# Attention and channel mix on one core: q, k and p laid out channels first, v as its tiles lie, and four output blocks stored channels first

## The chip, the core and the metric

The kernel runs on one core of a Trainium2 chip. The metric is the device time of one execution in microseconds. TensorE (PE) multiplies, VectorE (DVE) and ScalarE (ACT) do the elementwise work, GpSimd (POOL) sets constants, and SyncE (SP) issues nearly all transfers. Each engine works through its own queue in order; an instruction waits until the ones of other engines that it names are done.

## The reference

Eight batches of eight heads with 576 positions of 64 channels. Per head, 32 packed rows p attend to k and v; then q attends to what came out. The heads side by side (512 channels) go through a channel mix: two mixtures with the position before, one matrix with a squared ReLU and a second matrix behind it, and a sigmoid gate.

```python
def sm_attn(qq, kk, vv):
    s = scale * np.matmul(qq, kk.transpose(0, 1, 3, 2))
    a = np.exp(s - np.max(s, axis=-1, keepdims=True))
    a = a / (np.sum(a, axis=-1, keepdims=True) + 1e-09)
    return np.matmul(a, vv)
p_packed = sm_attn(p, k, v)
out = sm_attn(q, p_packed, p_packed)     # (8, 8, 576, 64) -> x (8, 576, 512)
xk = mu_k * x + (1.0 - mu_k) * x_prev    # x_prev: one position earlier
xr = mu_r * x + (1.0 - mu_r) * x_prev
k = np.maximum(xk @ w_k, 0.0)            # 512 -> 1024
v = k * k @ w_v                          # 1024 -> 512
r = 1.0 / (1.0 + np.exp(-(xr @ w_r)))
return (r * v).astype(np.float32)
```

## The kernel before

The 4608 positions are nine blocks of 512. A float32 product is made of three matmuls of a high and a low half: operand and weight are each split into two tiles (names ending in `h` and `l`). The first five blocks are done one by one (`gates`, `keys`, `values`: lines 1158 to 1160, 1091 to 1093, 1187 to 1189); the last four are two pairs, whose products come from sums and differences of quarters (`products_of`, line 1491), stored channels first on the chip and turned back before they are stored.

The attention of a batch runs in between. `front`: first scores of p and k (line 728; kT and qT hold two heads, channels on the partitions), maximum (801), exp (808), a turn of the weights by blocks of 32 with a way through memory (`weights_moved`, 851: `away`, then `aT`), weighted sum of v (750), pm (774) and its transpose (780). `scores` and `back`: second scores (884), softmax on DVE and ACT (900 to 923), product with pm (931), a copy into xt (954). Batch 0 has versions of its own (`first_side` and others, lines 568 to 663 and 977).

Loads before: q and k come in natural order. Batch 0's pairs of heads are transposed on PE (475, 506) and copied out by DVE and ACT (480, 483, 511, 514). For the other batches, four loads of 32 partitions with 32 channels each fill a `raw` tile (three of them), and DVE transposes it by 32 x 32 blocks into a `kq` tile (four of them, line 460). Positions are then in another order, which exp of batch 1 and the copy into xt undo. p goes the same way (533, 554). v comes in one or two, from batch 2 on in four loads for half a batch.

The weights are unpacked on the chip from 8-byte numbers (`convert`: ACT lines 342, 344, 356, DVE lines 347 and 358), 20 pieces.

What sets the order: the class `Flow` plays the program through while it is built, with estimated durations, and writes each engine's queue in the order in which steps become due; rank numbers decide between steps that are due (the table of numbers below). Tiles come from pools of slots (`take`, `give`): a step that takes a slot waits for the last user of it. Until the first gates are under way, `fill` puts matmuls of 128 columns on a constant into PE's queue wherever the play shows PE free (line 1859, tile `spare`).

The end: for a pair's output, DVE multiplies by the gate (1722, 1725), transposes by blocks (1732), and four stores per output tile of 128 channels write 32 x 16 x 32 pieces (`load`, line 245, is used for all transfers). The last tile of all is multiplied in two parts (1749), turned by PE (1756), copied by ACT and DVE (1760, 1763) and stored.

Of the kernel before, what the change touches and what calls it, by code (L numbers as in the profile page):

```python
# [8 lines left out]
F32 = mybir.dt.float32  # L9
# [4 lines left out]
AX = mybir.AxisListType  # L14

# [165 lines left out]

@with_exitstack
def attn_pack_channel_mix(ctx: ExitStack, tc: tile.TileContext, q, k, v, p, mu_k, mu_r, w_k, w_v, w_r, out):
    nc = tc.nc
    B, H, S, D = q.shape
    NP = p.shape[2]
    DM, DF = w_k.shape
    P = 128
    NG = H // 4
    NPR = H // 2  # L190
# [15 lines left out]
    FIRST = 12.453, 12.081, 16.585, 10.332  # L206
    RANK_1, RANK_MIX, RANK_KEYS, RANK_R, RANK_W, RANK_W2, RANK_V, LOADS_1, RANK_SQ, RANK_REST, HOLD_V, HOLD_S = 14.383, 2.279, 9.364, 21.382, 11.434, 11.544, 16.223, 19.391, 0.152, -6.533, 0.05, 0.25
    RANK_LATE1 = -1.021
    RANK_LATE2 = 7.09
    RANK_LATE3 = 9.434  # L210
    RANK_LATE4 = 10.248
    RANK_LATE5 = 2.56
    RANK_LATE6 = 9.599
    RANK_LATE7 = 3.494
    RANK_LATE8 = 20.327
    RANK_LATE9 = 10.578
    RANK_LATE10 = 7.095
    RANK_LATE11 = 3.446
    RANK_LATE13 = 29.829
    RANK_LATE14 = 4.595  # L220
    RANK_LATE12 = 8.964
# [30 lines left out]
    LATER, MARGIN = 1.2, 0.8  # L252
# [3 lines left out]
    def reached():  # L256
# [3 lines left out]
    RUNS = ((0, 5), (5, 5), (10, 4), (14, 4)), ((0, 4), (4, 4), (8, 5), (13, 5))  # L260
    MOVED = 2
    EARLY = 1
# [7 lines left out]
    BUFS = dict(raw=3, kq=4, vt=2, pt=1, a0=1, a1=1, aT=1, pm=2, e=3, a2=1, xt=6, tmp=4, xk=NC, sq=NF, sig=4,  # L270
                pa=2, both=1, m=4, n=4, staged=4, ex=3, pair=0, ring=0, store=4, twin=0)
# [7 lines left out]
    PAIRS = NB - 4, NB - 2  # L279
    MORE = {("sig", 4 + j): f"raw{j}" for j in range(3)}  # L280
    MORE.update({("sig", 7): "a20", ("tmp", 4): "ex2"})
    RANK_B, RANK_TURN, RANK_BACK, RANK_OUT, RANK_L = 0.2, 1.444, 1.061, 2.193, 44.75
    RANK_SUMS = dict(k=32.198, v=22.02, r=12.77)
    CHAINS = dict(A=(10.632, 0.893), B=(37.5, 6.511), R=(38.068, 6.0))
# [9 lines left out]
    for tag, n, size in (  # L294
        ("xk", NC, 2 * TB), ("sq", NF, 2 * TB), ("tmp", 4, WP), ("sig", 4, DM), ("kq", 4, S), 
        ("raw", 3, S), ("a2", 1, S), ("ex", 3, TB), ("e", 3, S), ("aT", 1, 5 * P), ("vt", 2, NPR * 5 * D),
    ):
        for j in range(n):
            sb.tile([P, size], F32, name=tag, tag=f"{tag}{j}")
# [71 lines left out]
    def first_pair(src, tag, j, space):  # L371

        slot = yield from flow.take(space)
        raw = tile_([P, 6, 2 * D], F32, space, slot, "raw")
        for hh in range(2):
            yield from load(
                raw[:T6, :, hh * D:(hh + 1) * D], src[0, 2 * j + hh].rearrange("(c p) d -> p c d", p=T6), 0.51, 0.6,
            )
            back_to_issue()
        if tag == "kT":  # L380
            flow.spawn(transposed_on_pe(tag, 0, j, space, slot, raw), RANK_LATE7 if j < 2 else RANK_LATE8, flow.free["dma"] + LANDS)
            return
        for hf in range(2):
            flow.spawn(
                first_transposed(j, hf, space, slot, raw), RANK_LATE9 if j < 2 else RANK_LATE10, flow.free["dma"] + LANDS
            )

    def first_loads():
        flow.spawn(first_packed(), 5)
        for h in range(2):  # L390
            for j in (2 * h, 2 * h + 1):
                flow.spawn(first_pair(k, "kT", j, "xk"), FIRST_K[h])
                flow.spawn(first_pair(q, "qT", j, "xk" if j == NPR - 1 else "sq"), FIRST_Q[h])
            flow.spawn(values_of(0, h), FIRST_V[h])

    def loads(b):
        flow.spawn(packed(b), lrank(b) - 0.03)
        for src, tag in ((k, "kT"), (v, "vt"), (q, "qT")):
            if tag == "vt":
                for h in range(2):  # L400
                    flow.spawn(values_of(b, h), lrank(b) - 0.01)
                continue
            flow.now.rank = lrank(b) - (0.02 if tag == "kT" else 0.0)
            for pr in range(NPR):

                space = "raw"
                slot = yield from flow.take(space)
                if b < EARLY:

                    raw = tile_([P, 6, 2 * D], F32, space, slot, "raw")  # L410
                    for hh in range(2):
                        yield from load(
                            raw[:T6, :, hh * D:(hh + 1) * D], src[b, 2 * pr + hh].rearrange("(c p) d -> p c d", p=T6),
                            0.51, 0.6,
                        )
                        back_to_issue()
                    flow.spawn(transposed_on_pe(tag, b, pr, space, slot, raw), rank(b), flow.free["dma"] + LANDS)
                    continue

                raw = tile_([P, NTB, 32], F32, "raw", slot)  # L420
                for o in range(0, P, 32):
                    hh, dh = divmod(o // 32, 2)
                    yield from load(
                        raw[o:o + 32],
                        src[b, 2 * pr + hh, :, 32 * dh:32 * dh + 32].rearrange("(t tb) d -> t tb d", tb=NTB),
                        0.63, 0.41,
                    )
                    back_to_issue()
                flow.spawn(transposed(tag, b, pr, slot, raw), rank(b) if b < 3 else RANK_TURN, flow.free["dma"] + LANDS + (LATER if b > 2 else 0.0))
# [4 lines left out]
    def values_of(b, h):  # L434

        slot = yield from flow.take("vt")
        vt = tile_([P, NPR, 5 * D], F32, "vt", slot)
        own = slice(h, H, 2) if b else slice(h * NPR, (h + 1) * NPR)
        if b < MOVED:
            yield from load(  # L440
                vt[:, :, :4 * D], v[b, own, :NQ, :].rearrange("h (p c) d -> p h (c d)", c=4), 0.46, 1.8
            )
            back_to_issue()
            yield from load(vt[:S - NQ, :, 4 * D:], v[b, own, NQ:, :].rearrange("h p d -> p h d"), 0.63, 0.45)
        else:

            own = v[b, h::2].rearrange("h (t tb) d -> t h (tb d)", tb=NTB)
            for j, (first, n) in enumerate(RUNS[h]):
                yield from load(vt[32 * j:32 * j + 32, :, :n * D], own[:, :, first * D:(first + n) * D], 0.46, 0.5)
                if j < 3:  # L450
                    back_to_issue()
        vts[b, h] = slot, vt
        flow.set(("vt", b, h))

    def transposed(tag, b, pr, raw_slot, raw):
        yield from reached()
# [35 lines left out]
    def first_transposed(pr, hf, raw_space, raw_slot, raw):  # L492
# [14 lines left out]
        if hf:  # L507
            flow.give(raw_space, raw_slot)
# [1379 lines left out]
```

## Time and profile before

| | |
|---|---|
| median of 3 runs | 570.71 us (570.67 to 571.06) |
| the profiled run's own time | 569.96 us |
| its span, first to last instruction | 567.8 us |
| PE, DVE, ACT busy | 98%, 83%, 67% of the span |
| first mixing matmul (line 1136) | 32.18 us |
| last matmul of the channel mix (line 1491) | starts at 560.96 us |
| DMA traffic | 86.16 MB, 229091 packets, 183848 of them under 512 B |

How to read it: the span runs from the first to the last instruction of the profiled execution, and all places below are microseconds from its start. In the profile an fp32 matmul of batch 0 or a filler appears as two records. The end of a matmul is modelled, so two that follow each other overlap in the rows; the distance between their starts is what one takes.

### The profile page before, as it was taken

What the parts mean: (1) busy time and instruction counts of PE and PEld (TensorE: products, weight loads), DVE (VectorE), ACT (ScalarE), POOL (GpSimd) and SP (SyncE); (2) the same over time, 40 slices, a digit from 0 to 9 for tenths busy, and PEclk for the clock granted to TensorE, in tenths of its full rate; (3) what the DMA queues carried; (4) which work ended last, traced back from release to release, by engine and by line L of the source; (5) the groups of instructions that cost most, each with busy time, mean ns of one, the idle gap of its engine ahead of it and who ended that gap; (6) DMA issues with size and microseconds to landing.
All of it is one profiled execution on the core that took longest, in us unless ns stands there. A gap on an engine that the chain in (4) does not pass through costs nothing.

```text
span 567.8 us, 10356 instructions
## 1 busy us (share of the span) xinstructions
PE 555.0 (98%) x3642; PEld 431.8 (76%) x3642; DVE 471.8 (83%) x926; ACT 378.8 (67%) x693; POOL 7.2 (1%) x36
## 2 busy tenths in 40 slices
PE   8999999999999999999999999999999999999995
PEld 7867767787787777677777777678888888888884
DVE  3797699937889988977998799994599997879874
ACT  2689979443585776365745668688996738787630
POOL 4000000000000000000000000000000000000000
PEclk9999999999999999999999999999999999999999
DMA  9989765666674865876747773242352483624255
GB/s 214 292 243 283 168 140 122 151 137 127 112 179 127 184 160 126 192 178 186 152 100 235 195 141 115 100 147 75 102 194 63 120 208 77 202 75 148 80 124 94
DMA packets 229091, 86.16 MB, mean 152 GB/s; under 512 B 183848, under 2 KB 217136, under 8 KB 229040
## 3 DMA queue, kind: packets, MB, share of 16 engines
q1 hardware_dynamic: 224624, 84.58, 59.3%
q10 hardware_dynamic: 4160, 0.66, 0.6%
q8 instruction: 29, 0.48, 0.4%
q0 software_dynamic: 256, 0.26, 0.2%
q14 instruction: 22, 0.18, 0.1%
HBM read 62.00 MB, written 23.46 MB: 151 GB/s over the span
## 4 chain that ended last, share of the span: by engine, by line
PE 61%; DVE 19%; ACT 7%; DMA 6%; SPq 4%; issue 3%; DVEq 0%; ACTq 0%
PE ph L1491 31%; SPq L245 4%; PE ph L1091 3%; PE ph L1092 3%; PE ph L1093 3%; PE pvo L1187 3%; PE pvo L1189 3%; PE pvo L1188 3%; DVE x L1058 3%; DMA raw<-in_k 2%; PE pr L1158 1%; PE pr L1159 1%; PE pr L1160 1%; DVE sw L1326 1%; DVE sig L1198 1%
## 5 line engine op out<-in xcount | busy, mean ns | idle before, releaser
L1187 PE MATMUL pvo<-wv_h,sq 128*128 128x512 f32 x160 | 64.4, 403 | 0.2 <-ACT r L1103 0.2
L1091 PE MATMUL ph<-xk,wk_h 128*128 128x512 f32 x160 | 64.4, 402 | 0.0
L1188 PE MATMUL pvo<-wv_l,sq 128*128 128x512 f32 x160 | 62.4, 390 | 0.0
L1092 PE MATMUL ph<-xk,wk_h 128*128 128x512 f32 x160 | 62.4, 390 | 0.0
L1093 PE MATMUL ph<-xk,wk_l 128*128 128x512 f32 x160 | 62.4, 390 | 0.0
L1189 PE MATMUL pvo<-wv_h,sq 128*128 128x512 f32 x160 | 62.4, 390 | 0.0
L954 ACT COPY xt<-pa 128x576 f32<-128x576 f32 x28 | 33.0, 1258 | 15.7 <-PE pa L931 15.7
L1491 PE MATMUL ph<-vT,ring 128*128 128x512 f32 x174 | 43.0, 393 | 0.0
L1058 DVE SCALAR_TENSOR_TENSOR x<-xt,mus,x 128x64 f32<-128x64 f32 (+5 forms) x80 | 34.9, 475 | 6.5 <-ACT x L1054 6.5
L1187 PEld LDWEIGHTS pvo<-wv_h,sq 128*128 128x128 f32 x160 | 30.0, 188 | 12.6 <-issue 5.0
L1054 ACT ACTIVATE x<-xt,mus 128x64 f32<-128x64 f32 (+5 forms) x80 | 35.6, 500 | 5.5 <-DVE sq L1112 2.6
L1103 ACT ACTIVATE r<-ph 128x512 f32<-128x512 f32 x40 | 23.8, 596 | 22.4 <-PE ph L1093 15.8
L1491 PEld LDWEIGHTS ph<-vT,ring 128*128 128x128 f32 x174 | 32.7, 188 | 7.4
L1091 PEld LDWEIGHTS ph<-xk,wk_h 128*128 128x128 f32 x160 | 30.1, 188 | 10.8 <-issue 4.1
L1189 PEld LDWEIGHTS pvo<-wv_h,sq 128*128 128x128 f32 x160 | 30.0, 188 | 6.5
L1093 PEld LDWEIGHTS ph<-xk,wk_l 128*128 128x128 f32 x160 | 30.0, 188 | 6.5
L1188 PEld LDWEIGHTS pvo<-wv_l,sq 128*128 128x128 f32 x160 | 30.1, 188 | 5.6
L1092 PEld LDWEIGHTS ph<-xk,wk_h 128*128 128x128 f32 x160 | 30.1, 188 | 5.6
L1491 PE MATMUL ph<-vB,wv_h 128*128 128x512 f32 x104 | 32.4, 393 | 0.0
L1342 ACT CAST sw<-sw 128x256 fp32r<-128x256 f32 x40 | 15.5, 403 | 20.1 <-DVE sw L1326 8.9
L1344 DVE TENSOR_TENSOR sw<-sw 128x256 fp32r<-128x256 f32 x40 | 16.3, 416 | 15.1 <-ACT sw L1342 15.1
L1110 DVE CAST sq<-r 128x512 fp32r<-128x512 f32 x40 | 16.5, 413 | 13.6 <-ACT r L1106 13.1
(224 smaller groups left out, 1383.0 us busy)
## 6 DMA issues: line engine op xcount, KB each, us to landing
sum<-sw SPq DMA_DIRECT2D x40, 256.0 KB, 2.5
ring<-sum SPq DMA_DIRECT2D x36, 256.0 KB, 3.2
raw<-in_k SPq DMA_DIRECT2D x112, 72.0 KB, 2.8
raw<-in_q SPq DMA_DIRECT2D x112, 72.0 KB, 2.9
out<-sig SPq DMA_DIRECT2D x20, 256.0 KB, 2.7
wv_h<-sum SPq DMA_DIRECT2D x18, 256.0 KB, 3.5
wv_l<-sum SPq DMA_DIRECT2D x18, 256.0 KB, 4.0
st<-in_moe_w_k SPq DMA_DIRECT2D x8, 512.0 KB, 5.6
```

Source lines behind the costliest of these rows:

```text
L245: dict(queue=nc.sync, scalar=nc.scalar, gpsimd=nc.gpsimd)[queue].dma_start(dst, src)
L954: nc.scalar.copy(*in_order(b, xt[:, :, 1 + hf * HS:1 + (hf + 1) * HS], xt[:, :, 1:].rearrange("p c (t a b) -> p c a b t", a=2, t=32)[:, :, ...
L1054: nc.scalar.mul(x32[:, o:o + n], xts[b, c][:, 1 + s:1 + s + n], mus[:, j, c:c + 1])
L1058: nc.vector.scalar_tensor_tensor(x32[:, o:o + n], xts[b, c][:, s:s + n], mus[:, j + 1, c:c + 1], x32[:, o:o + n], op0=ALU.mult, op1=ALU.add,)
L1091: nc.tensor.matmul(ph, wk_h[:, c, fs], xh, start=(c == 0), stop=False)
L1092: nc.tensor.matmul(ph, wk_h[:, c, fs], xl, start=False, stop=False)
L1093: nc.tensor.matmul(ph, wk_l[:, c, fs], xh, start=False, stop=(c == NC - 1))
L1103: nc.scalar.activation(r, ph, AF.Relu)
L1187: nc.tensor.matmul(pv[t], sh, wv_h[:, f, :], start=(n == 0), stop=False)
L1188: nc.tensor.matmul(pv[t], sh, wv_l[:, f, :], start=False, stop=False)
L1189: nc.tensor.matmul(pv[t], sl, wv_h[:, f, :], start=False, stop=(n == NF - 1))
L1491: nc.tensor.matmul(bank[2], w, x, start=(not more and step == k == 0), stop=(step == 2 and k == count - 1), skip_group_check=True,)
```

## The change

The arrays are laid out before the launch, and put together after it. q and k are passed as (8, 4, 128, 576): two heads' channels on the partitions; p as (8, 128, 128); v by half of the heads in the order of the tiles; the shares of mu_k and mu_r by channel. On the chip, kT and qT are loaded as they are used, one load each, into `kq` (seven tiles; `raw` is gone). The transposes of q, k and p on PE and DVE, and the copies behind them, are taken out. pt is loaded for batch 0 in two loads into a zeroed tile. Positions stay in natural order, so exp and the copy into xt write plain rows. v's half batch is one load of 128 rows and one of 64. The last four blocks are stored channels first, one store per tile of 128 channels; the transposes at the end are taken out. The table of ranks has other numbers, and with the count RANK_LATE13 all 20 weight pieces take the other branch of `convert`: ACT's first step goes, and DVE's one step becomes two.

```diff
-    FIRST = 12.453, 12.081, 16.585, 10.332
-    RANK_1, RANK_MIX, ... = 14.383, 2.279, 9.364, 21.382, 11.434, 11.544, 16.223, 19.391, 0.152, -6.533, 0.05, 0.25
-    RANK_LATE13 = 29.829
+    FIRST = 19.125, 23.858, 15.496, 14.378
+    RANK_1, RANK_MIX, ... = 14.138, 6.204, 10.067, 22.577, 16.168, 18.235, 23.505, 24.159, 0.05, -0.644, 0.056, 0.212
+    RANK_LATE13 = 0.991
...
-    BUFS = dict(raw=3, kq=4, vt=2, ...
+    BUFS = dict(kq=7, vt=2, ...
...
+    def turned(src, tag, b, pr):
+        slot = yield from flow.take("kq")
+        t = tile_([P, S], F32, "kq", slot, tag)
+        yield from load(t, src[b, pr], 0.46, 1.0)
...
-                raw = tile_([P, NTB, 32], F32, "raw", slot)
-                for o in range(0, P, 32):
-                    hh, dh = divmod(o // 32, 2)
-                    yield from load(raw[o:o + 32],
-                        src[b, 2 * pr + hh, :, 32 * dh:32 * dh + 32].rearrange("(t tb) d -> t tb d", tb=NTB), ...
+        for pr in range(NPR):
+            flow.spawn(turned(k, "kT", b, pr), lrank(b) - 0.02)
...
-        yield vec(S)
-        nc.vector.transpose(t.rearrange("p (a b) -> p a b", b=32), raw)
...
+        main = v[b, h, :4 * P * NPR * D].rearrange("(p c r d) -> p c r d", p=P, c=4, r=NPR)
+        yield from load(vt[:, :4], main, 0.46, 1.8)
...
-        nc.scalar.copy(*in_order(b, xt[...], xt[...].rearrange("p c (t a b) -> p c a b t", a=2, t=32)[:, :, hf], px))
+        nc.scalar.copy(xt[:, :, 1 + hf * HS:1 + (hf + 1) * HS], px[:, :, :HS])
...
-        nc.vector.transpose(x.rearrange("p (b i) -> p b i", i=32), sig)
-        for a in range(4):
-            yield from load(out[t0:t0 + TB, d * P + 32 * a:d * P + 32 * a + 32]..., x[32 * a:32 * a + 32]..., 0.63, 0.4, queue)
+        yield from load(out[b * TB + d * P:b * TB + (d + 1) * P, :], sig, 0.46, 0.9, queue)
...
-            nc.tensor.transpose(turned[:, at:at + P], sig[:, part.start + at:part.start + at + P], ident)
-            nc.scalar.copy(x, turned)
+        yield from load(out[t0:t0 + P, part], sig[:, part], 0.4, 0.3, "queue" if part.start else "scalar")
```

PE's queue at the start of the program, before the change (`spare` is a filler, `pa<-ident,raw` and `pq<-ident,raw` are transposes of k and q, `pa<-kT,pt` the first scores, `pa<-ident,a` the turn of the weights, `pv` the weighted sum):

```order
L1859 MATMUL spare<-ident 128x128 x10
L475 MATMUL pa<-ident,raw 128x96 x6
L1859 MATMUL spare<-ident 128x128 x3
L475 MATMUL pa<-ident,raw 128x96 x6
L1823 MATMUL pu<-ident,rows 128x8
L1859 MATMUL spare<-ident 128x128
L506 MATMUL pq<-ident,raw 128x96 x3
L568 MATMUL pa<-kT,pt 64x288 x4
L506 MATMUL pq<-ident,raw 128x96 x6
```

The same place with the change:

```order
L1681 MATMUL spare<-ident 128x128 x12
L441 MATMUL pa<-kT,pt 64x288 x4
L1681 MATMUL spare<-ident 128x128 x10
L687 MATMUL pa<-ident,a 128x128 x4
L688 MATMUL pa<-ident,a 64x128
L1681 MATMUL spare<-ident 128x128 x5
L462 MATMUL pv<-vt,aT 32x64 x20
L1681 MATMUL spare<-ident 128x128 x2
L483 MATMUL pT<-ident,pm 128x128
L441 MATMUL pa<-kT,pt 64x288 x4
L496 MATMUL pa<-both,qT 128x64 x10
```

The transposes are gone and fillers stand in their places; up to the first mixing matmul there are 43 fillers before and 61 with the change. Batch 1's first scores move up from behind the 13th group of three gates matmuls to behind the first, and all of batch 1's front stands ahead of the keys.

SP's queue in the body, before the change, where the loads of k for one batch follow the stores of weight sums:

```order
L245 DMA raw<-in_k 32x18x32 x4
L245 DMA vt<-in_v 32x4x320 x2
L245 DMA vt<-in_v 32x4x256 x4
L245 DMA vt<-in_v 32x4x320 x2
L245 DMA raw<-in_q 32x18x32 x6
```

The same with the change (the fourth kT of a batch and its qT come apart from the first three kT):

```order
L247 DMA vt<-in_v 128x1024
L247 DMA vt<-in_v 64x256
L247 DMA vt<-in_v 128x1024
L247 DMA vt<-in_v 64x256
L247 DMA sum<-sw 128x512 x2
L247 DMA out<-sig 128x512
L247 DMA kT<-in_k 128x576
L247 DMA qT<-in_q 128x576 x2
```

The fourth kT waits for PE's second scores of the batch before; on PE 24 matmuls of the channel mix stand between those and the batch's own first scores in five of six cases, 30 in the other.

SP's queue at the end, before the change:

```order
L245 DMA wv_h<-sum 128x2x256
L245 DMA wv_l<-sum 128x2x256
L245 DMA out<-turn 32x16x32
L245 DMA out<-x 32x16x32 x4
L245 DMA out<-x_6053 32x16x32 x4
L245 DMA out<-x_6083 32x16x32 x4
L245 DMA out<-turn 32x16x32 x2
L245 DMA out<-turn 128x128
```

And with the change:

```order
L247 DMA wv_h<-sum 128x2x256
L247 DMA wv_l<-sum 128x2x256
L247 DMA out<-sig 128x512 x2
L247 DMA out<-sig 128x128
```

Sixteen stores behind the last weight sums become three on this queue (four more, of 128 x 512 and 128 x 384, are on ACT's).

## Rows read from the trace of the kernel before

**Rows 1.** The page's first part: busy us, share of the span, instructions
```profile
PE 555.0 (98%) x3642; PEld 431.8 (76%) x3642; DVE 471.8 (83%) x926; ACT 378.8 (67%) x693; POOL 7.2 (1%) x36
```

**Rows 2.** PE in order of time: start, duration in us, line, operation, out<-in
```profile
205.42 0.39 PE L1188 MATMUL pvo<-wv_l,sq 128*128 128x512 f32 x1
205.65 0.39 PE L1189 MATMUL pvo<-wv_h,sq 128*128 128x512 f32 x1
```

**Rows 3.** Waits of PE: for whom, us in total, times, longest
```profile
PE pa L780 <- DVE pm L774: 1.5, 2, 1.3
PE pa L728 <- DVE kT L460: 1.3, 2, 0.9
PE pa L931 <- DVE a L923: 0.9, 2, 0.5
...
PE pa L977 <- DVE xr L990: 0.5, 1, 0.5
```

**Rows 4.** PE in order of time, first 33 us
```profile
1.60 4.63 PE L1859 MATMUL spare<-ident 128*128 128x128 f32 x20 [1.60 <-POOL ident masks.py:199]
6.03 0.81 PE L475 MATMUL pa<-ident,raw 96*128 96x96 f32 x6
...
15.37 1.19 PE L568 MATMUL pa<-kT,pt 128*64 128x288 f32 x8
16.49 0.33 PE L610 MATMUL pT<-ident,pm 128*128 128x128 f32 x1
...
17.18 2.44 PE L623 MATMUL pa<-both,qT 128*128 128x64 f32 x20
...
19.96 0.67 PE L822 MATMUL pa<-ident,a 128*128 128x128 f32 x4
...
20.58 1.73 PE L1859 MATMUL spare<-ident 128*128 128x128 f32 x14
22.23 0.90 PE L589 MATMUL pv<-vt,aT 128*32 128x64 f32 x40
...
26.75 0.66 PE L656 MATMUL pa<-ident,e 112*128 112x112 f32 x5
...
28.23 1.99 PE L977 MATMUL pa<-a2t,mub 64*128 64x512 f32 x8
30.15 2.27 PE L1859 MATMUL spare<-ident 128*128 128x128 f32 x18
32.18 0.47 PE L1136 MATMUL pr<-wr_h,xr 128*128 128x512 f32 x1
```

**Rows 5.** DVE's groups by line and shape: busy us, mean ns, idle before
```profile
L460 DVE STREAM_TRANSPOSE kT<-raw 128x576 f32<-128x576 f32 x28 | 20.8, 762 | 2.8 <-PE pa L884 2.8
...
L1110 DVE CAST sq<-r 128x512 fp32r<-128x512 f32 x40 | 16.5, 413 | 13.6 <-ACT r L1106 13.1 <-PE pvo L1189 0.4
...
L347 DVE SCALAR_TENSOR_TENSOR m<-m,st 128x512 uint32<-128x512 uint32 x20 | 13.3, 673 | 1.1 <-ACT m L344 1.1
```

**Rows 6.** Busy us (instructions) of PE, PEld, DVE, ACT, POOL from 33 to 50
```profile
33.00:50.00 17.00, 16.48 (x92) 10.24 (x98) 15.28 (x25) 15.09 (x30) 0.10 (x1) 1.00 0.98 276
```

**Rows 7.** DVE and SP in order of time after the last matmul
```profile
561.38 0.75 DVE L1749 TENSOR_TENSOR sig<-ph,sig 128x384 f32<-128x384 f32 x2 [1.35 <-PE ph L1491]
...
562.24 3.15 SPq L245 DMA_DIRECT2D out<-turn  x3
```

**Rows 8.** Waits of SP's queue from 548 us on: total us, times, longest
```profile
SPq L245 <- DMA out<-turn: 3.8, 2, 1.9
```

**Rows 9.** Transfers of the whole run: count, KB each, median us to landing
```profile
out<-sig SPq DMA_DIRECT2D x20, 256.0 KB, 2.7
...
st<-in_moe_w_r SPq DMA_DIRECT2D x4, 512.0 KB, 6.5
...
out<-turn SPq DMA_DIRECT2D x27, 64.0 KB, 1.9
```

More of the change, by code (lines that the diff above doesn't have):

```diff
@@ L179, in run, with runs_of_blocks, attn_pack_channel_mix @@
         assert not stuck, stuck
+def runs_of_blocks(n):
+    n, more = divmod(n, 4)
+    sizes = [n + 1] * more + [n] * (4 - more), [n] * (4 - more) + [n + 1] * more
+    return tuple(tuple((sum(s[:j]), s[j]) for j in range(4)) for s in sizes)
 @with_exitstack
-def attn_pack_channel_mix(ctx: ExitStack, tc: tile.TileContext, q, k, v, p, mu_k, mu_r, w_k, w_v, w_r, out):
+def attn_pack_channel_mix(ctx: ExitStack, tc: tile.TileContext, q, k, v, p, mu_k, mu_r, mu_by_channel, w_k, w_v, w_r, out):
     nc = tc.nc
-    B, H, S, D = q.shape
-    NP = p.shape[2]
+    B, NPR, P, S = q.shape
+    D = P // 2
+    H = 2 * NPR
+    NP = p.shape[2] // NPR
     DM, DF = w_k.shape
-    P = 128
     NG = H // 4
-    NPR = H // 2
     HS = S // 2
@@ L369, in lrank @@
         return LOADS_1 if b == 1 else rank(b) if b < 3 else RANK_L + 0.2 * b
[L371 to L386, printed above, removed]
+    def turned(src, tag, b, pr):
+        slot = yield from flow.take("kq")
+        t = tile_([P, S], F32, "kq", slot, tag)
+        yield from load(t, src[b, pr], 0.46, 1.0)
+        ts[tag, b, pr] = slot, t
+        flow.set((tag, b, pr))
     def first_loads():
@@ L397, in loads @@
         flow.spawn(packed(b), lrank(b) - 0.03)
[L398 to L418, printed above, removed]
-                raw = tile_([P, NTB, 32], F32, "raw", slot)
-                for o in range(0, P, 32):
-                    hh, dh = divmod(o // 32, 2)
[L423 to L429, printed above, removed]
+        for pr in range(NPR):
+            flow.spawn(turned(k, "kT", b, pr), lrank(b) - 0.02)
+        for h in range(2):
+            flow.spawn(values_of(b, h), lrank(b) - 0.01)
+        for pr in range(NPR):
+            flow.spawn(turned(q, "qT", b, pr), lrank(b))
+        yield from flow.wait(*(("qT", b, pr) for pr in range(NPR)))
     def back_to_issue(queue="queue"):
@@ L436, in values_of @@
         slot = yield from flow.take("vt")
[L437 to L451, printed above, removed]
+        vt = tile_([P, 5, NPR, D], F32, "vt", slot)
@@ L533, in packed @@
-        nc.vector.transpose(pt, pin)
+        yield from load(pt, p[b].rearrange("p (r n) -> p r n", n=NP), 0.46, 0.25)
         pts[b] = slot, pt
@@ L616, in first_side @@
         flow.spawn(first_shares(h, pm), RANK_MIX - 0.1)
-        yield from flow.wait(*(("qT", 0, j, hf) for j in (j0, j0 + 1) for hf in range(2)))
+        yield from flow.wait(("qT", 0, j0), ("qT", 0, j0 + 1))
         slot = yield from flow.take("pa")
@@ L1117, in first_gates @@
     def first_gates():
-        yield from flow.wait(*(("qT", 0, j, hf) for j in range(NPR) for hf in range(2)), ("xr", 0, 0))
+        yield from flow.wait(*(("qT", 0, j) for j in range(NPR)), ("xr", 0, 0))
         opened = []
@@ L1261, in spaces @@
             feed_ring("two", ("kq", one), ("kq", two))
-        for _ in range(3):
-            yield from flow.take("raw")
         for j in range(3):
+            one = yield from flow.take("kq")
+            MORE["sig", 4 + j] = f"kq{one}"
             flow.give("sig", 4 + j)
@@ L1813, in shares @@
     def shares():
[L1814 to L1817 removed]
+        for j in range(2):
+            yield from load(mus[:, 2 * j], mu_by_channel[:, j], 0.46, 0.02, "scalar")
             if not j:
                 back_to_issue("scalar")
[L1820 to L1825 removed]
         yield vec(2 * NC)
[L1827 to L1830 removed]
+        nc.vector.tensor_scalar(mus[:, 1::2, :], mus[:, 0::2, :], -1.0, 1.0, op0=ALU.mult, op1=ALU.add)
         flow.set("mu")
```

254 lines of the change are left out of this document (77 added, 177 removed).

## The prediction

> **What bounds the kernel now.** I read the page's first part, then the order of TensorE's work in time, then who made it wait. PE is busy 98% of the span, DVE 83%, ACT 67% [rows 1]. A PE busy time can hide gaps, so the next thing to see is the distance between starts: a 512-column matmul is booked at 0.39 us, but the next starts 0.23 us after it, each on the heels of the one before [rows 2]; a booked end lies 0.16 us behind the slot. Some 2050 such matmuls stand in the program, 465 us of the 568. They stay. What can move is therefore small and has three places: the stretch before the first mixing matmul at 32.18 us [rows 4], the waits of PE in the body, and what follows the last matmul.
>
> In the body PE waits little, and for DVE: 1.5 us for pm, 1.3 us for a turned kT, 0.9 us for a, and 0.5 us for an xr [rows 3]; these four are 4.2 us.
>
> At the end DVE's two parts of the last product run from 561.38 to 562.13, but the last three stores are issued from 562.24 to 565.39 [rows 7]: SP waited 3.8 us for earlier `out<-turn` stores to land before it could issue the next ones [rows 8]. From the end of the last issue to the end of the span are 567.8 - 565.4 = 2.4 us.
>
> **The change part by part.** The sum is made against the profiled run's own 569.96 us (span 567.8 and 2.2 us around it); the median of the runs shown, 570.71, is 0.75 above it.
>
> *The head.* All 48 batch-0 transposes on PE go (L475, L506), with the one of the shares (L1823). But PE's queue is written ahead of time, and the changed order has 61 filler matmuls ahead of the first mixing matmul where 43 stood. So the head is a sum of PE slots again. The first 10 fillers take 6.03 - 1.60 = 4.43 us at the start, 0.44 us each; later a group of 14 records (7 fillers) takes 22.23 - 20.58 = 1.65 us, 0.236 us each and about half as long; 51 of them are 12.0 us [rows 4]. Then, from the same rows: two first scores of 16.49 - 15.37 = 1.12, two groups of five transposes of 20.58 - 19.96 = 0.62, two weighted sums of 0.90 - 0.16 = 0.74, two turns of pm of 0.17, two second scores of 2.44 - 0.16 = 2.28, the five transposes of e of 0.50, the four mixing products of 30.15 - 28.23 = 1.92: 2.24 + 1.24 + 1.48 + 0.34 + 4.56 + 0.50 + 1.92 = 12.3 us. The first mixing matmul would start at 1.60 + 4.43 + 12.0 + 12.3 = 30.3 us, against 32.18: 1.9 us earlier. This is the floor of the head, if nothing is late. The chain beside it (first scores, maximum, exp, turn, sum) is shorter by its transposes and their evacuations, about as long as the fillers that stand for it. Two things can be later than the fillers: the first kT and pt, which now come in whole rows but with pt in pieces, and pm, for which two fillers (0.47 us) now stand between sum and turn. I put 0.3 and 0.2 us on them, and one filler pair less follows: a gain of 1.4 + 0.2 = 1.6 us; bounds 2.1 us of gain and 0.5 us of loss.
>
> *DVE in the body.* 56 blockwise transposes of k and q leave it, 0.76 us each, 28 of them 20.8 us [rows 5], with those of the outputs and of p; its total was 471.8 us [rows 1]. Against that, the conversion of the 20 weight pieces gets a third DVE step (L350) where ACT did one before (the count RANK_LATE13 falls from 29.8 to 0.99). Its price is not in the trace: the nearest rows are a cast of the same size, 0.413 us, and the two-input step beside it, 0.673 us [rows 5]; I take 0.5, nearest to the one-input cast, 20 x 0.5 = 10 us, ends 8 and 13.5, none of it on the path by itself. The Trainium skill's page "VectorE: DVE Perf Modes" (The perf-mode tier table) gives a one-input tensor_scalar in fp32 twice the rate of a two-input op, 1227 ns for 2048 elements; the estimate from that page is 0.31 us and 6 us in all. DVE is some 32 us lighter over the body. The three waits for DVE, 3.7 us, are late arrivals of a queue that was full, and most of them go; kT's goes by construction, since no DVE step makes it. I take 3.0 us of gain. Bounds: 3.7 us, and 2.2 us of loss, if two new waits as long as the old ones for kT and a arise. ACT's rearranging copies (exp of batch 1, xt) become plain, and the conversions take one ACT step less; ACT was off the path, so nothing for that.
>
> *Loads.* Four loads of k or q with 128-byte runs become one of 288 KB with 2304-byte rows; v's eight become four; SP issues 328 instead of 591 transfers. Loads no longer wait for three raw tiles that DVE empties, but for seven kq tiles that PE empties. The price is weighed under the rivals. I take nothing.
>
> *The end.* After DVE's last product (562.13) the PE transposes, the ACT and DVE copies and the strided stores go; each output block is one store. SP waits for no earlier small store. The last store, issued at about 562.2 for 0.4 us, then ends the span 2.4 us later: 565.0, a gain of 2.8 us. A 256 KB store landed in 2.7 us where a 64 KB one took 1.9 [rows 9]; if the larger last pieces cost that difference, the gain is 2.0. I take 2.6, bounds 1.5 (one wait for an earlier store stays) and 3.2. The Trainium skill's page "DMA: Bandwidth & Descriptors" (Anatomy of one DMA) says that about 2.0 us of any transfer are fixed, mostly the receipt of its last byte, and do not scale with size; by that the layout saves nothing on the last store itself, and an estimate with its 436 GB/s for the 192 KB piece is 2.0 + 0.45 = 2.45 us, a gain of 2.2 us in the end and 0.4 us less in the sum. The trace agrees as to the small slope, 1.9 against 2.7 us for four times the bytes [rows 9].
>
> **The sum:** 1.6 + 3.0 + 2.6 = 7.2 us. 569.96 - 7.2 = 562.8 us for the profiled run, 563.5 us for the median.
>
> **The rivals.**
> 1. *Only the end gains.* PE's fillers and order in the head are fixed, so data that land late or a DVE that is busier there (the third conversion step) eat the head, and new waits replace the old. In the dense stretch before the keys DVE was busy 15.28 of 17.00 us [rows 6]; it held 6 conversion steps L347 and 4 turned kT. Six further steps of 0.41 to 0.67 are 2.5 to 4.0 us, the four transposes that go 3.1 us: between 0.6 us less and 0.9 us more in 1.7 us of slack. So DVE fits on average, but batch 1's whole front now stands in that stretch and its pm stands behind the conversions in DVE's queue. For it: that placing. Against: the slack, and 30 us less afterwards. Time: 569.96 - 2.6 + 0.75 = 568.1 us.
> 2. *PE waits for kT (slower).* A batch's last kT load can be issued only when the second scores of the batch before have given a kq tile back, and the first scores that need it stand only 24 matmuls behind those on PE: 24 x 0.227 = 5.4 us. A 256 KB transfer took 2.7 us, so it fits; a w_r load that queued behind others took 6.5 us [rows 9]. Six batches (2 to 7) can wait. The gain of 7.2 us is gone when the load lands 5.4 + 7.2/6 = 6.6 us after the scores; at 7.5 us the cost is 6 x 2.1 = 12.6 us and the time 563.5 + 12.6 = 576 us. For it: SP's queue is in order, with stores that wait for DVE ahead of that load, and the v loads (576 KB each) go just before. Against: the transfers after the weights are shorter, and far fewer are issued.
> 3. *All waits go.* With the bounds of all three terms, 2.1 + 3.7 + 3.2 = 9.0 us: 561.7; without the 0.5 us for xr, 561.2 us.
> 4. *No change:* the head loses what the end gains (its bound 0.5 and two new waits of 2.2 in the body against 2.6): about 570.8 us.
>
> **How the numbers follow.** The forecast has 0.66 (with its bounds 561.2 to 567, where one or two new waits are left), rival 1 has 0.18, rival 2 has 0.06, a time below 561.2 (rival 3 and shorter) 0.06, rival 4 has 0.04. The range of 560.5 to 567.7 takes in the forecast, most of rival 3 and half of rival 1, and leaves out less than 2 in 10. About 0.2% (1.1 us) is what a measurement of this kernel can tell from no change: faster 0.90 (forecast, rivals 1 and 3), same 0.04 (rival 4), slower 0.06 (rival 2).
>
> **What would show it.** Head: the first mixing matmul at 30 to 31 us; later than 32.2, and fillers or data were mis-sized. Body: no PE wait for a kT made by DVE, the waits for pm and a together under 1 us; a wait of the first scores for `kT<-in_k` would be rival 2, and one for pm of batch 1 near 50 us rival 1. End: the last store issued within 0.3 us of DVE's last product and the span over 3 us later; a wait of SP for an earlier store there would be the part that I left at 1.5. If the spacing of 0.227 us itself changes, the whole frame is wrong.

## The result, and the profile after

The changed kernel takes 563.38 us (median of six runs, 561.01 to 564.64), the kernel before 570.88 us beside it. The ratio is 0.9858, 95% interval 0.9834 to 0.9882: 7.5 us or 1.4% faster. The profiled run is the shortest of the six, 561.01 us with a span of 558.9; this matters below.

The page's first part and its DMA line after the change (busy us, share of the span, instructions):

```profile
PE 550.4 (98%) x3623; PEld 430.5 (77%) x3623; DVE 430.1 (77%) x857; ACT 349.0 (62%) x664; POOL 7.2 (1%) x36
...
DMA packets 57135, 86.10 MB, mean 154 GB/s; under 512 B 6272, under 2 KB 33024, under 8 KB 57088
```

Beside [rows 1], DVE lost 41.7 us, ACT 29.8 us and PE 4.6 us, and packets under 512 B fell from 183848 to 6272. How much of that is time is told by three marks on PE: the first mixing matmul, the last matmul, the end of the span.

| | before | after | gain |
|---|---|---|---|
| first mixing matmul starts, us | 32.18 | 32.57 | -0.39 |
| from there to the start of the last matmul | 528.78 | 522.30 | 6.48 |
| from there to the end of the span | 6.86 | 3.99 | 2.87 |
| span | 567.82 | 558.86 | 8.96 |

The head, as PE's work in order of time (start, duration in us, line, operation, idle before and what ended it); this answers [rows 4]:

```profile
1.59 5.14 PE L1681 MATMUL spare<-ident 128*128 128x128 f32 x24 [1.59 <-POOL ident masks.py:199]
8.48 1.19 PE L441 MATMUL pa<-kT,pt 128*64 128x288 f32 x8 [1.75 <-DMA qT<-in_q]
9.60 2.50 PE L1681 MATMUL spare<-ident 128*128 128x128 f32 x20
...
28.84 1.99 PE L839 MATMUL pa<-a2t,mub 64*128 64x512 f32 x8
...
32.57 0.47 PE L998 MATMUL pr<-wr_h,xr 128*128 128x512 f32 x1
```

After twelve fillers PE stands idle for 1.75 us before the first scores. The tile named there (qT) is the profile's guess: these matmuls read kT and pt. The second half of p landed at 8.35 us, 0.13 us ahead of them, while both kT were there at 4.48. The transfers issued in the first 4 us (KB each, median us to landing) show the load that is late:

```profile
kT<-in_k SPq DMA_DIRECT2D x2, 288.0 KB, 3.1
...
pt<-in_p ACTq DMA_DIRECT2D x2, 32.0 KB, 6.1
```

The waits of PE after the change (for whom, us in total, times, longest), all there are:

```profile
PE pa L441 <- DMA qT<-in_q: 1.7, 1, 1.7
PE spare L1681 <- POOL ident masks.py:199: 1.6, 1, 1.6
PE pa L839 <- DVE xr L852: 0.5, 1, 0.5
PE pa L623 <- DVE xk L852: 0.5, 1, 0.5
PE pvo L1049 <- ACT r L965: 0.2, 1, 0.2
PE pr L1509 <- DVE sig L1060: 0.2, 1, 0.2
```

Those for pm, kT and a of [rows 3] are gone. The two for DVE's line 852 lie at 45.66 and 51.21 us, ahead of the first keys matmul, where batch 1's front now stands.

The end, first PE and DVE, then the two issuing queues (the last issue of each ends where its group ends):

```profile
554.87 0.39 PE L1353 MATMUL ph<-wk_h,wv_l 128*128 128x512 f32 x1
...
555.30 0.76 DVE L1599 TENSOR_TENSOR sig<-ph,sig 128x384 f32<-128x384 f32 x2 [2.09 <-PE ph L1353]
...
548.45 8.00 SPq L247 DMA_DIRECT2D out<-sig  x3
...
553.24 2.99 ACTq L247 DMA_DIRECT2D out<-sig  x2
```

SP's last issue ends at 556.45, 0.39 us after DVE's last product; the span ends 2.4 us later, as it did before. In [rows 7] the distance from DVE's last product to the end of SP's last issue was 565.39 - 562.13 = 3.26 us.

### The profile page after: what moved, and what is told of

Its sections match the earlier page's. It is cut to its first block, busy times and chain, and to the rows that moved or that the text cites. A ratio compares the mean times of both kernels' runs of the same rounds, so it can differ in the third digit from the quotient of the medians.

```text
span 558.9 us, 9836 instructions
## 1 busy us (share of the span) xinstructions
PE 550.4 (98%) x3623; PEld 430.5 (77%) x3623; DVE 430.1 (77%) x857; ACT 349.0 (62%) x664; POOL 7.2 (1%) x36
## 4 chain that ended last, share of the span: by engine, by line
PE 83%; DVE 11%; ACT 2%; issue 2%; DMA 1%; DVEq 0%; ACTq 0%
PE ph L1353 31%; PE pvo L1049 6%; PE ph L953 6%; PE pvo L1050 5%; PE pvo L1051 5%; PE ph L954 5%; PE ph L955 5%; PE pr L1020 3%; PE pr L1021 3%; PE pr L1022 3%; PE pa L796 2%; PE pa L623 1%; DVE m L352 1%; PE pr L1509 1%; PE pr L1511 1%
## 5 line engine op out<-in xcount | busy, mean ns | idle before, releaser
L965 ACT ACTIVATE r<-ph 128x512 f32<-128x512 f32 x40 | 23.9, 598 | 39.5 <-PE ph L955 29.8
L1353 PE MATMUL ph<-vT,ring 128*128 128x512 f32 x156 | 38.7, 393 | 0.0
L1353 PE MATMUL ph<-vB,wv_h 128*128 128x512 f32 x112 | 34.8, 392 | 0.0
L1353 PEld LDWEIGHTS ph<-vT,ring 128*128 128x128 f32 x156 | 29.3, 188 | 6.6
L920 DVE SCALAR_TENSOR_TENSOR chain<-xt,mus,chain 128x448 f32<-128x448 f32 (+6 forms) x40 | 20.4, 535 | 17.3 <-ACT chain L916 17.1
L1031 ACT ACTIVATE sig<-pr 128x512 f32<-128x512 f32 x28 | 16.4, 600 | 21.5 <-PE pr L1022 11.3
L974 DVE TENSOR_TENSOR sq<-r,sq 128x512 fp32r<-128x512 f32 x40 | 27.2, 683 | 0.2
```

What stands on the lines that cost most here:

```text
L920: nc.vector.scalar_tensor_tensor(x32[:, o:o + n], xts[b, c][:, s:s + n], mus[:, j + 1, c:c + 1], x32[:, o:o + n], op0=ALU.mult, op1=ALU.add,)
L965: nc.scalar.activation(r, ph, AF.Relu)
L974: nc.vector.tensor_tensor(hl[:, 1, :], r, hl[:, 0, :].bitcast(F32), op=ALU.subtract)
L1353: nc.tensor.matmul(bank[2], w, x, start=(not more and step == k == 0), stop=(step == 2 and k == count - 1), skip_group_check=True,)
```

## Experiments

The runs came in four groups, with the kernel before beside each (median 570.3 to 571.1 us); between groups the ratios to it are compared. Of the body, the stretch from the first keys matmul (line 953) to the last matmul is used, summed from the distances between PE's starts, since the planner puts the fillers and batch 1's front in different places ahead of it: 507.90 us before, 496.33 us after. Of the 11.57 us between them 3.8 is work that stands ahead of the keys after the change (32 second scores of batch 1, 80 products of its weighted sums, 11 transposes, by their own distances); 7.8 us are waits.

### The head: the changed kernel again, p in rows, and the idle time covered

**The changed kernel again**, nothing edited.

> The changed kernel as it is, timed again beside the others. In its profiled run the first mixing matmul started at 32.57 us (before: 32.18), from there to the last matmul it took 522.3 us (before: 528.8) and from there to the end 4.0 us (before: 6.9). That run took 561.0 us at a granted clock of 1.0; the other five took 562.8 to 564.6 at 0.993 to 0.997. Theory A: the wait of PE in the head (1.75 us from 6.73 us on, for the late rows of p) is where the clock is lost, so most runs are again near 563.4 at 0.996, a run at 1.0 is near 561.0, and a profile with the lower clock shows the stretch at the lower level in the first 20 us. Theory B: the clock is lost elsewhere in the body, so such a profile shows the stretch behind 33 us. If all runs are at 1.0 and 563, the clock is no part of it.

Median 563.04 us (561.42 to 564.34); its one run at clock 1.0 is the one of 561.42. The profiled run took 563.26 us. PE in its head, then the stretches of 1 us (busy us of PE, PEld, DVE, ACT, POOL, then the granted clock of PE, DMA share, GB/s):

```profile
1.59 4.87 PE L1681 MATMUL spare<-ident 128*128 128x128 f32 x24 [1.59 <-POOL ident masks.py:199]
9.15 2.19 PE L441 MATMUL pa<-kT,pt 128*64 128x288 f32 x8 [2.69 <-DMA pt<-in_p]
11.27 3.07 PE L1681 MATMUL spare<-ident 128*128 128x128 f32 x20
...
34.80 0.47 PE L998 MATMUL pr<-wr_h,xr 128*128 128x512 f32 x1
```

```profile
8.00:9.00 1.00, 0.00 (x0) 0.00 (x0) 0.00 (x0) 0.00 (x0) 0.00 (x0) 1.00 1.07 334
9.00:10.00 1.00, 0.85 (x4) 0.60 (x6) 0.00 (x0) 0.00 (x0) 0.00 (x0) 0.54 0.98 277
10.00:11.00 1.00, 1.00 (x6) 0.27 (x2) 0.00 (x0) 0.00 (x0) 0.00 (x0) 0.50 0.97 361
11.00:12.00 1.00, 1.00 (x5) 0.73 (x4) 0.62 (x1) 0.00 (x0) 0.00 (x0) 0.50 0.70 274
12.00:13.00 1.00, 1.00 (x9) 1.00 (x8) 0.62 (x4) 0.57 (x1) 0.00 (x0) 0.75 0.72 164
```

p came 0.7 us later than in the first profile; PE was idle for 2.69 us in place of 1.75, and when it started again the clock was at its lower level (0.50, 1.2 GHz) in the next rows. The same first scores took 2.19 us in place of 1.19. The first mixing matmul is at 34.80 in place of 32.57: 0.67 us by the later start and 1.56 us by the clock. The body is the same to 0.1 us (522.26). So the 561.01 of the first profile is the good case of the changed kernel, and theory A holds.

**p in rows.** One load of 128 rows, zeros in place:

```diff
-        nc.gpsimd.memset(pt, 0.0)
-        for hh, half in enumerate(HALVES):
-            yield from load(pt[half, :, hh], p[0, half]..., 0.5, 0.1, "scalar")
...
+        yield from load(pt.rearrange("p r a n -> p (r a n)"), p_first, 1.0, 0.2, "scalar")
```

> One part of the head: p of batch 0 is passed with its zeros in place, so one load of 128 rows of 1 KB takes the place of two loads in runs of 128 bytes behind a memset. The order of all queues stays. Theory A (the late p alone delays the head): the first scores start at 6.7 us in place of 8.48, the first mixing matmul at 30.8 in place of 32.57, and the time is 1.7 us below the changed kernel at clock 1.0 (559.3), or 4 us below it in the median if the clock is lost at that wait. Rival: the chain behind (softmax, conversions of the gate's weights) is as late, a wait of 1 to 1.75 us shows up elsewhere before the first mixing matmul, and the time is within 0.5 us of the changed kernel.

Median 558.78 us (558.44 to 559.32), 4.3 us below the changed kernel beside it; ratio to before 0.9782 (0.9762 to 0.9803). PE, and the load:

```profile
1.48 5.49 PE L1677 MATMUL spare<-ident 128*128 128x128 f32 x24 [1.48 <-POOL ident masks.py:199]
6.90 1.30 PE L437 MATMUL pa<-kT,pt 128*64 128x288 f32 x8
...
31.09 0.47 PE L994 MATMUL pr<-wr_h,xr 128*128 128x512 f32 x1
```

```profile
pt<-in_p_first ACTq DMA_DIRECT2D x1, 128.0 KB, 3.9
```

Theory A holds: the first scores start at 6.90 us and the idle time is gone, and with it the spread of the runs (0.9 us in place of 2.9). No other wait took its place in the head. Four times the bytes per load land in 3.9 us in place of 6.1; the load is also issued earlier, at 0.73 us in place of 1.25 and 1.97, since no memset stands before it. The Trainium skill's page "DMA: Bandwidth & Descriptors" (Rules for kernel authors) says that two transfers to disjoint partition halves share the same engines, and that one of 128 partitions should be used; the trace agrees, with 3.9 against 6.1 us. This edit also made the runs longer and the issue earlier, so it does not show what each of the three is worth.

**The idle time covered.** The changed kernel with 11 more fillers ahead of the first scores; p is as late as ever.

```diff
         s1 = banks(slot)
+        for _ in range(0 if h else 11):
+            flow.fill()
```

> The changed kernel with 11 more fillers of 128 columns on PE right ahead of the first scores, nothing else: the engine works where it stood idle (11 x 0.236 = 2.6 us from 6.5 us on), and p lands as late as before. Theory A (the idle wait itself takes the clock): the granted clock stays at 1.0, the first scores start at 9.1 to 9.3 us, the first mixing matmul at 33.3, and all runs are at 561.5 to 561.9, 1.4 us below the changed kernel's median of 563.0. Rival (the clock falls for another cause, or the late p delays more than PE): the clock falls in 8 to 15 us all the same, median 563 or above.

Median 561.71 us (561.35 to 562.38), ratio 0.9842 against 0.9854 for the changed kernel; the intervals (0.9819 to 0.9866 and 0.9831 to 0.9878) overlap, so the medians alone don't decide. The clock does: 0.999 to 1.0 in all four runs, where five of six runs of the changed kernel had 0.993 to 0.997. PE in the head:

```profile
1.59 7.58 PE L1683 MATMUL spare<-ident 128*128 128x128 f32 x46 [1.59 <-POOL ident masks.py:199]
9.11 1.19 PE L443 MATMUL pa<-kT,pt 128*64 128x288 f32 x8
```

The first scores start as late as in the slow profile above (9.11 and 9.15), yet take 1.19 us, and the first mixing matmul is at 33.20. So the clock's part of the loss comes from the idle wait, not from the late data. The Trainium skill's page "TensorE: Matmul & The Clock Gate" (HAM oscillation) describes just this, a stage that begins at the slow clock after a wait for a transfer; these three runs agree.

### The end

The last four blocks are turned on the chip and stored in natural order again:

```diff
...
+        yield vec(TB)
+        nc.vector.transpose(x.rearrange("p (b i) -> p b i", i=32), sig)
...
+        for a in range(4):
...
+            yield from load(out[t0:t0 + TB, d * P + 32 * a:...], x[32 * a:32 * a + 32]..., 0.63, 0.4, queue)
...
-        yield from load(out[b * TB + d * P:b * TB + (d + 1) * P, :], sig, 0.46, 0.9, queue)
```

> The end undone: the last four blocks are turned on the chip and stored in natural order as before, all else as changed. Theory A (the end is worth what follows the last matmul): from the last matmul to the end 6.9 us in place of 4.0, time 2.8 us above the changed kernel (about 566.2), body and head the same. Rival: the blockwise transposes and the many stores of the pairs also made the body's waits, so it is 4 us or more above; or the stores' landing hides the difference, under 1 us.

Median 566.19 us, 3.15 us above the changed kernel; in the profile the stretch behind the last matmul is 6.73 us (3.99 without the edit), and the body is the same (522.28). SP's waits at the end are back, as in [rows 8]:

```profile
SPq L247 <- DMA out<-turn: 4.2, 2, 2.4
```

The end is worth 2.7 us by the trace, and nothing of the body came from it.

### The numbers: conversions and ranks

**The other branch of the conversion.** On the kernel with p in rows, `RANK_LATE13 = 29.829` in place of 0.991: ACT does the first step again.

> On the kernel with p in rows (558.8 us): the count RANK_LATE13 is 29.829 again, so all 20 weight pieces take the branch of before (ACT does a first step, DVE one step less; the third DVE step took 0.42 us here, 8.4 us in all). Theory A (the prediction's: the third DVE step is on no path): within 0.5 us of 558.8, first mixing matmul within 0.5 us of 31.1, body within 0.5 us of 522.3. Rival (DVE is the last in the head, busy 5.9 of 6 us from 20 to 26): first mixing matmul 0.5 to 1.5 us earlier and the time with it.

Median 557.70 us (557.65 to 557.99), 1.1 us lower; ratio to before 0.9772 (0.9749 to 0.9795), against 0.9782: 0.6 us, with intervals that overlap, so the times alone don't decide. By the traces the last matmul starts 1.67 us earlier: 0.37 us at the first mixing matmul, 0.4 from there to the first keys matmul, 0.9 behind it. So the rival holds in size, though most of it lies behind the head; 33 to 57 us is where DVE was relieved. That stretch with p in rows, and then with this edit; below them PE's waits with it:

```profile
33.00:57.00 24.00, 22.89 (x222) 14.38 (x208) 19.12 (x38) 19.39 (x40) 0.10 (x1) 1.00 0.65 211
```

```profile
33.00:57.00 24.00, 23.20 (x211) 14.81 (x211) 15.87 (x29) 22.73 (x47) 0.10 (x1) 1.00 0.66 217
```

```profile
PE spare L1677 <- POOL ident masks.py:199: 1.5, 1, 1.5
PE pa L649 <- DVE pm L643: 0.3, 1, 0.3
PE pa L619 <- DVE xk L848: 0.3, 1, 0.3
```

DVE has 3.2 us less to do there. The wait for xr is gone, that for xk is 0.3 us in place of 0.5, and one of 0.3 us for pm is new. The third DVE step of the changed kernel costs some 1 us on the path: 0.6 by the ratios, 1.1 by the medians, 1.7 by the two profiled runs, of which the first was the longest of its five.

**The old ranks** on the kernel with p in rows: all rank numbers that both kernels have.

> On the kernel with p in rows (558.8 us): all rank numbers that both kernels have are set to those of before (RANK_LATE13 among them), the layout stays as changed. The head's fillers grow with it (109 ahead of the first mixing matmul in place of 61), so only the stretch behind it is compared. Theory A (the body's gain of 6.5 us came from the layout): from the first mixing matmul to the last matmul 522 to 523.5 us. Rival (it came from the order that the new numbers give): 525 to 529 us, with waits of PE for pm, a or xr back. The head: 48 more fillers of 0.236 us less what they displace, 5 to 11 us later.

Median 564.93 us. The head has 89 fillers ahead of the first mixing matmul, which starts at 40.10 us. The body is 519.0 us, less than expected, since part of batch 1 stands ahead of it; from the first keys matmul on it is 496.33 us, to the hundredth that of the changed kernel. But this edit brings ACT's branch of the conversion back too, and with that branch and the new numbers the stretch took 495.48 us. So at most 0.9 of the body's 11.57 us can come from the new numbers; they serve the head. Setting only the body's numbers back, with ACT's branch:

> On the kernel with p in rows and ACT's branch of the conversion (557.7 us, body 521.0): the rank numbers of the body (rank of the batches, sums of weights, chains) are those of before, the head's stay. With the whole old table the body was 519.0 us, but the head 9 us longer, with part of batch 1 in it. Theory A (the old numbers are as good in the body; what was shorter there stood in the head): time within 0.7 us of 557.7. Rival (the new numbers of the body cost something): 555.5 to 557.

557.86 us (557.54 to 558.55), the same as without: theory A.

### The body: what the layout of q and k removed

Batches 1 to 7 get DVE's transposes back, or the four loads, or the small runs, alone and together. The DVE step works in place on the loaded tile, and the host lays q and k so that the result is the same:

```diff
...
+            blocks = t.rearrange("p (a b) -> p a b", b=32)
+            nc.vector.transpose(blocks, blocks)
```

> One part undone in the body: each kT and qT of batches 1 to 7 is laid out by blocks again and passes DVE, which transposes it in its place (56 steps of about 0.76 us, 43 us in all); loads, tiles and the end stay as changed. Theory A (the body's 6.5 us came from a lighter DVE): PE's waits for pm, a and kT return, the stretch from the first mixing matmul to the last matmul grows by 3 to 6.5 us, time 566 to 570. Rival (the gain came from fewer and larger loads and from the order): the stretch stays within 1 us of 522.3 and the time within 1 us of the changed kernel.

The next pair has the four loads without a DVE step, the second of them with rows of 2304 bytes. The two have the same order in every queue:

```diff
-        yield from load(t, src[b, pr], 0.46, 1.0)
+        if not b:
+            yield from load(t, src[b, pr], 0.46, 1.0)
...
+            for o in range(0, P, 32):
...
+                yield from load(blocks[o:o + 32], rows[b, 2 * pr + hh, :, 32 * dh:32 * dh + 32]..., 0.63, 0.41)
...
```

> On the kernel with p in rows (558.8 us, body 522.3 us): k and q of batches 1 to 7 come in four loads each with runs of 128 bytes as before the change, but the DVE transposes behind them are left out (so the scores of those batches are of mixed-up channels and positions; sizes and all other work are the same). With both, loads and transposes, the body was 532.5. Theory A (after the two runs: DVE's steps are 3 to 4 us of the body, the small runs the rest): body 525 to 529 with waits of PE or ACT that lead back to a transfer, clock 1.0 unless a wait of over 2 us stands in it. Rival (loads cost only because DVE's step stands behind each): body within 1 us of 522.3.

> The same with the same order in every queue, but each of the four loads reads 32 rows of 2304 bytes (channels first, as in the changed kernel; nothing left out). Theory A (small runs cost, not the number of transfers that SP issues): body 521.5 to 523.5, time within 1 us of 558.8. Rival (it is SP's queue of four times the issues): body as with the runs of 128 bytes.

The last pair has four loads and the DVE step, with small runs and with long rows, again in one order:

> On the kernel with p in rows (558.8 us): k and q of batches 1 to 7 come as before the change, in four loads each of 32 partitions with runs of 128 bytes, and are transposed by DVE in their place (56 steps); tiles, order numbers and end stay as changed. The run with the DVE step alone had a body of 526.0 us in place of 522.3. Theory A (DVE's load alone made the waits, loads are hidden): body 525.5 to 526.5, time 562 to 566. Rival (small runs and SP's issues were the rest of the 6.5 us): body 527.5 to 530, with waits of PE for kT, and time 565 to 569.

> The partner of the run with both loads and transposes back (571.1 us, 568.0 to 574.2): the order of every queue is the same, four loads for each kT and qT and a DVE step behind each, but each load reads 32 rows of 2304 bytes (k and q laid out by blocks, channels first) in place of runs of 128 bytes. So far, waits of PE between the first keys matmul and the last matmul beyond those of the changed kernel: 7.8 us before the change, 1.6 with DVE's steps alone, 0.8 with the small runs alone, 0.1 with four loads alone, 7.9 with small runs and DVE's steps. Theory A (small runs and DVE's steps add up because a tile that lands late is then transposed late): waits 1 to 3 us, time 562 to 566. Rival (four issues with a DVE step behind each are enough, by the stores that stand behind them on SP): waits 6 to 9 us, time 568 or more.

| batches 1 to 7 | median, us | first keys to last matmul | work that stands there in addition | waits beyond the changed kernel |
|---|---|---|---|---|
| before the change | 570.88 | 507.90 | 3.8 | 7.8 |
| DVE step, one load | 569.36 | 499.03 | 1.1 | 1.6 |
| four loads, long rows | 562.19 | 499.01 | 2.6 | 0.1 |
| four loads, small runs | 564.28 | 499.69 | 2.6 | 0.8 |
| four loads, long rows, DVE step | 567.02 | 505.29 | 2.6 | 6.4 |
| four loads, small runs, DVE step | 571.08 | 506.85 | 2.6 | 7.9 |

The medians hold more than the waits: the planner counts longer loads and puts up to 16 more fillers ahead (78 in all, against 62, in the pair without the DVE step), and the run with one load and the DVE step was built on the late p. So the last column is compared, from one profiled run each; that of the last row took 568.78 us, 2.3 less than its median. The stretches from the first mixing matmul, of which the expectations speak, hold 8 to 19 fillers more (0.23 us each). The last two rows also hold a loss by the clock, shown below, of some 1.7 us each: their waits alone are 4.7 and 6.2 us.

For the DVE step alone the stretch from the first mixing matmul grew by 3.7 us, 2.1 of it fillers: the truth lies between theory A and the rival. Four loads with long rows make 0.1 us of waits, as their theory A has it; their time missed its forecast by being 3.4 us above 558.8, for which the 16 fillers (3.7 us) are enough.

For the small runs alone the rival's 1 us holds behind the first keys matmul, but not ahead of it. From the first mixing matmul to the last that run took 529.33 us, its partner with long rows and the same order 526.33, and 2.3 of these 3.0 us stand ahead of the keys. There ACT waits for a weight load, and PE for ACT; the load was issued at 35.16 us and landed at 43.04, with long rows at 31.81 and 38.92. The clock falls behind PE's waits of 0.93 and 0.58 us, though the expectation had asked for one of over 2 us:

```profile
43.12 0.66 ACT L344 ACTIVATE m<-st 128x512 f32<-128x512 f32 x1 [1.25 <-DMA st<-in_moe_w_k]
...
44.30 0.50 PE L1005 MATMUL pr<-wr_h,xr 128*128 128x512 f32 x1 [0.93 <-ACT xr L857]
```

```profile
47.00:49.00 2.00, 2.00 (x8) 0.77 (x6) 1.95 (x4) 1.32 (x3) 0.00 (x0) 0.50 0.64 176
```

Neither part alone makes the waits of before; four loads with a DVE step behind each make 6.4 us, small runs 1.5 us more (4 us by the ratios, 1.0004 against 0.9933). The run with small runs and the DVE step lies above both of its forecasts: 532.51 us from the first mixing matmul, 8 more fillers among them. In the last run theory A fell; the rival's waits came (6.4 us), its time not quite (567.02), and its cause, stores that stand on SP, is not what the trace shows for long rows. How it happens is seen in two places. With long rows, DVE, then ACT, then PE:

```profile
331.58 0.77 DVE L386 STREAM_TRANSPOSE qT<-qT 128x576 f32<-128x576 f32 x1
...
335.51 0.73 DVE L386 STREAM_TRANSPOSE qT<-qT 128x576 f32<-128x576 f32 x1
336.17 0.72 DVE L791 TENSOR_TENSOR e<-e,m 128x576 f32<-128x576 f32 x1
336.81 1.41 DVE L675 TENSOR_REDUCE mx<-pa 128x1 f32<-128x576 f32 x2
...
338.31 0.74 ACT L681 ACTIVATE a<-pa,nmx 128x576 f32<-128x576 f32 x1 [2.60 <-DVE nmx L677]
...
340.76 0.74 ACT L681 ACTIVATE a<-pa,nmx 128x576 f32<-128x576 f32 x1
...
341.65 1.09 PE L803 MATMUL pa<-a,pm 32*64 32x288 f32 x8 [1.55 <-ACT a L681]
```

```profile
342.00:344.00 2.00, 2.00 (x11) 1.14 (x4) 2.00 (x6) 2.00 (x6) 0.00 (x0) 0.50 0.31 121
```

DVE works without a gap; the maxima stand behind three transposes of qT, ACT waits 2.60 us for the first of them, and PE 1.55 us for ACT's second exp. Behind that the clock is at its lower level. With small runs it goes through SP instead:

```profile
337.26 0.60 ACT L976 ACTIVATE r<-ph 128x512 f32<-128x512 f32 x1 [3.50 <-DMA sum<-sw]
...
337.91 0.58 PE L1060 MATMUL pvo<-wv_h,sq 128*128 128x512 f32 x1 [2.37 <-ACT r L976]
...
338.71 0.63 PE L1062 MATMUL pvo<-wv_h,sq 128*128 128x512 f32 x1
339.14 0.63 PE L1060 MATMUL pvo<-wv_h,sq 128*128 128x512 f32 x1
```

```profile
338.00:339.00 1.00, 1.00 (x3) 0.82 (x4) 1.00 (x3) 1.00 (x3) 0.00 (x0) 0.60 0.00 0
339.00:340.00 1.00, 1.00 (x4) 0.71 (x4) 0.98 (x4) 1.00 (x3) 0.00 (x0) 0.50 0.00 0
```

A store of weight sums stands behind sixteen small-run loads of q on SP; it was issued at 334.68 us and landed at 337.18, where with long rows the same store was issued at 330.84 and landed at 333.02. SP takes 0.63 us (median) to issue a small-run load and 0.42 us with long rows. By the profile ACT waits for the store, PE waits for ACT, and behind the wait the clock is at its lower level: matmuls start 0.43 us apart in place of 0.23. What stays open is why one load with a DVE step makes only 1.6 us: its planned order differs too, and that was not separated. Nor was it tested by itself what v's larger loads and ACT's plain copies are worth.

## Why the prediction was right, and where it was not

The time was 563.38 us against 563.5, but the terms were not that good: three misses cancel (the head, the body, and the distance of the median from the profiled run), and that they do is luck.

- **The head** was to gain 1.6 us (bounds: 2.1 us of gain, 0.5 us of loss): it lost 0.4 us in the profiled run and 2.6 us in the second one, where the clock fell. The sum of PE slots was sound: with p in rows the first mixing matmul came at 31.09, against 30.3 us for the floor and 30.6 forecast. The step that failed is the 0.3 us for "the first kT and pt, which now come in whole rows but with pt in pieces". pt came 1.75 to 2.7 us after the fillers, and the clock's fall behind such a wait had no term and no place in the bounds.
- **The body** was to gain 3.0 us, 3.7 at most; it gained 6.5 us (7.8 behind the first keys matmul, less 1.3 ahead of it). Two steps failed. The bound was the sum of the waits listed for DVE [rows 3], 3.7 us, but a booked matmul ends 0.16 us behind its slot, as the prediction itself had read, so each listed wait is too short, and short ones are not listed: the kT waits listed with 1.3 us are 2.1 us by distances of starts. And the "I take nothing" for the loads left out that a load with a DVE step behind it costs more than either alone, and that small runs keep SP longer at each issue (0.63 against 0.42 us).
- **The third DVE step** was sized well (0.5 us taken, 0.42 measured) and put on no path; it costs 0.6 to 1.7 us there. The row:

```profile
L350 DVE TENSOR_SCALAR m<-m x20: 364/420/428, 22.3 to 87.7; 128x512 uint32<-128x512 uint32 x20
```

  From the Trainium skill's page "VectorE: DVE Perf Modes" (The perf-mode tier table) the prediction had estimated 0.31 us, a quarter of the 1227 ns for 2048 elements; the measurement decides.
- **The end** was to gain 2.6 us; it gained 2.9, and 2.7 by the experiment. The last store's 2.4 us behind its issue did not change, as the prediction took it. The 192 KB piece landed 1.9 us after its issue and the last one, of 64 KB, 1.8. The section of the Trainium skill's page "DMA: Bandwidth & Descriptors" (Anatomy of one DMA) from which the prediction estimated 2.45 us is on transfers that GpSimd issues; ACT issued this one.
- **The median** was put 0.75 us above the profiled run; it lies 2.4 us above, because the profiled run kept the full clock and most others did not.

The sum for the profiled run was 7.2 us and is 8.95; the clock gave 1.6 us back. Of the rivals, the first was partly there: the 0.5 us waits for xr and xk in the stretch with batch 1's front, and DVE's conversions behind them. The second, PE waiting for kT, did not come: the loads landed in a median of 4.5 us where the 24 matmuls leave 5.4, and no wait for a kT is among PE's waits.

A version that beats both follows from the runs: p in rows with ACT's branch of the conversion, 557.70 us, 2.3% below the kernel before; by the ratios (0.9772 against 0.9858) that is 4.9 us below the changed one.

## What to carry to other kernels

Read lost time on a busy engine from the distances between starts, and take the listed waits as a floor. When loads are re-laid, look at the first one that the first real work needs: a small load in short runs, issued beside large ones, decides when the chain starts. And price a load together with what stands behind it on its engine and its queue; put back apart, the two parts made waits of 0.8 and 1.6 us behind the first keys matmul, together 7.9, 1.7 of it by the clock.

## What the hardware showed that was not expected

- The clock fell to its lower level within the head after PE had been idle for 2.69 us, and not after 1.75 us of idling in another run of the same kernel; in the run with long rows and the DVE step it fell behind a wait of 1.55 us, and in the one with small runs alone behind waits of 0.93 and 0.58 us, so the length of one wait does not tell alone. The loss behind it was 1.56 us in the head. Fillers over the same stretch kept it at 1.00.
- Two loads of 32 KB in runs of 128 bytes landed in 6.1 us beside loads of 288 and 512 KB in long rows; one load of 128 KB in rows of 1 KB, issued 0.5 us ahead of the first of those, landed in 3.9 us.
- With four loads and a DVE step each, the same bytes in runs of 128 bytes in place of 2304 cost 4 us by the ratios (medians 571.08 and 567.02) under the same order of every queue, and spread the runs over 6 us (568.0 to 574.2) in place of 1.2. SP took 0.63 us to issue one such load and 0.42 us with long rows.
